# Evacuating the keys by two ScalarE operations, one directly copied head, and later stores of the first query block

## The chip, the cores and the metric

The kernel runs on one core of one Trainium2 chip. The metric is the device time of one execution in microseconds, the median of several runs. Below, PE is TensorE, DVE is VectorE, ACT is ScalarE, POOL is GpSimd, and SP is the engine whose queue issues almost all DMAs of this kernel.

## The reference

A gated mix of multi-query attention and a SwiGLU feed-forward on the same input, all in float32:

```python
def _A_ref(x, wq, wk, wv, wo):                 # 2048 tokens, 32 heads of 16, one key/value head
    q = transpose((x @ wq).reshape(B, S, H, Dh), 0, 2, 1, 3)
    k = x @ wk
    v = x @ wv
    scores = einsum("bhqd,bkd->bhqk", q, k) * (Dh ** -0.5)
    o = einsum("bhqk,bkd->bhqd", softmax(scores, -1), v)
    return transpose(o, 0, 2, 1, 3).reshape(B, S, H * Dh) @ wo

def _B_ref(x, w_gate, w_up, w_down):           # 512 -> 1792 -> 512
    return (silu(x @ w_gate) * (x @ w_up)) @ w_down

g = sigmoid((x * gate_w).sum(-1, keepdims=True))
return g * _A_ref(x, ...) + (1 - g) * _B_ref(x, ...)
```

x has 2048 rows of 512.

## The kernel before, in words

**Split numbers.** Most matmuls run in the chip's rounded float32 type. Each operand is split into a high part (the rounded value) and a low part (the rest), and a product is three matmuls: high by high, low by high, high by low. So a projection of 512 tokens (a chunk `c`; there are four) to 128 columns is 12 matmuls of 128x128 by 128x512, accumulated in one bank of PSUM, a tile `pf` of which there are three.

**The opening.** For each chunk `transpose_x` loads x, transposes it on PE (16 small matmuls per half chunk) into a PSUM tile `pss`, and splits it into `xh` (ACT) and `xl` (DVE). `project_kv` projects the chunk on keys, values and the gate together, on 113 output partitions. The key appears several times, because scores are also made of split parts: in `ks`, partitions 0 to 47 and 64 to 111 hold high, high, low of the keys, and partitions of ones hold -1. The values and the gate go through `vz` and a transposition (`transpose_v`) into `vaug`. `nk` collects the largest size of each key component, and `spread_k` brings it by one matmul into `kmax`; a query row times `kmax` bounds its scores, so that the softmax needs no maximum of its own.

**The query projection** goes in four blocks `m` of 128 columns (eight heads). `query(m, c)` makes the 12 matmuls, and its `keep` takes the bank out as `hh` (high), `hl` (low) and `qb` (the bound, size times `kmax`), and stores the three to DRAM (`q_d`). Block 0 is projected before the loop over heads begins. For the heads in `QS`, in the kernel before heads 0 and 1, their 16 rows of each part are also copied straight from these tiles into `qs`, the tile from which the scores are made, four copies for each head and chunk. The other heads are read back from `q_d` by `load_head`.

**The loop over heads** (`score`, `mix`) goes over 512 units (head by key tile of 128). A unit takes 4 score matmuls of 64 rows (two run beside each other), two exponentials of 128x1024 on ACT, and 8 small matmuls that multiply by the values. Between them PE works off a queue of jobs, cut in halves of 64 rows: eight steps for every two units, in this order: the queries of blocks 1 to 3, then the feed-forward (gate, up, down), then output parts. What is left after the loop is done at full width. `fill(GAP)` makes some of these jobs at full width before the loop: it takes jobs of 12 matmuls until GAP is used up.

**What sets the order.** Within the opening and the loop the order is as written; each engine works its instructions in program order and waits by semaphores. SP's queue is in order too: a DMA whose source is not ready holds those behind it. Two engines that read one PSUM tile do so one after the other, by waits that the compiler adds. Loads of weights that stand between the two regions are placed by a scheduler, and so may be issued earlier than they are written. `load_split` loads a weight into one of two `wraw` buffers and POOL splits it.

Of the kernel before, what the change touches and what calls it, by code (L numbers as in the profile page):

```python
# [8 lines left out]
F32 = mybir.dt.float32  # L9
F32R = mybir.dt.float32r  # L10
BF16 = mybir.dt.bfloat16
I32 = mybir.dt.int32
AF = mybir.ActivationFunctionType
# [5 lines left out]
P = 128  # L19
# [20 lines left out]
SPOT = 16  # L40
SLACK = 6
LONG = 8
GAP = 24
RATE = 8
FIRST = 5
STOP = 5
# [5 lines left out]
def tile_gated_mix(ctx, tc, x, wq, wk, wv, wo, w_gate, w_up, w_down, gate_w, out):  # L52
# [48 lines left out]
    def mm(ps, terms):  # L101
        n = len(terms)
        for i, (a, b) in enumerate(terms):
            nc.tensor.matmul(ps, a, b, start=(i == 0), stop=(i == n - 1))  # L104
# [7 lines left out]
    def run(queue, n):  # L112
        for _ in range(min(n, len(queue))):
            queue.pop(0)()
# [68 lines left out]
                run(LOADS, 2)  # L183


    WQ, QS = {}, {}

    def load_wq(m):
        WQ[m] = load_split(wq_v[:, :, m * P:(m + 1) * P], f"wq{m}", 1, qpool)

    def query(m, c):
        cs = slice(c * CH, (c + 1) * CH)
        t = m * NCH + c

        def terms():
            r = []
            for k in range(KD):
                r += three(WQ[m], XC[c], (slice(None), k), (slice(None), k))
            return r

        def keep(ps):
            qh = wp.tile([P, CH], F32R, name="hh", bufs=7)
            ql = wp.tile([P, CH], F32R, name="hl", bufs=7)

            qb = wp.tile([P, CH], F32, name="ht", bufs=2)
            if m:
                nc.vector.tensor_copy(qh, ps)
            else:
                nc.scalar.activation(qh, ps, AF.Copy)
            nc.vector.tensor_tensor(ql, ps, qh.bitcast(F32), ALU.subtract)  # L210
            if m:
                nc.vector.tensor_scalar(qb, qh.bitcast(F32), kmax, None, op0=ALU.mult)
                nc.vector.scalar_tensor_tensor(qb.bitcast(F32R), qb, -1.0, qb, op0=ALU.mult, op1=ALU.max)
            else:
                nc.scalar.activation(qb.bitcast(F32R), ps, AF.Abs, scale=kmax)
            parts = [ql, qh, qb.bitcast(F32R)]
            if not m:
                for h, qs in QS.items():
                    for i, part in enumerate([qh] + parts):
                        row = c % 2 * RT + i * DH  # L220
                        nc.sync.dma_start(qs[row:row + DH, c // 2, :].bitcast(F32), part[h * DH:(h + 1) * DH].bitcast(F32))  # L221
            for j, part in enumerate(parts):
                nc.sync.dma_start(q_d[m * HG:(m + 1) * HG, j * DH:(j + 1) * DH, cs], part.bitcast(F32))  # L223
            nc.vector.tensor_reduce(top[:, t:t + 1], qb, axis=AX.X, op=ALU.max)

        return Job(3 * KD, lambda: m in WQ, terms, keep)
# [127 lines left out]
    def whole(job):  # L354
        for i in range(job.size):
            job.step(i)
        run(ACTS, 1)
# [109 lines left out]
    def new_qs(h):  # L467
        QS[h] = qsp.tile([P, 2, CH], F32R, name="qs")
        return QS[h]

    with tc.tile_pool(name="apool", bufs=1) as ap, tc.tile_pool(name="apool2", bufs=2) as a2:
# [35 lines left out]
            nc.vector.memset(vaug[:, :, DH:], 1.0)  # L507

        nc.gpsimd.memset(ks.bitcast(F32), -1.0)
        nk = ap.tile([DH, 2 * NCH + 1], F32, name="nk")  # L510
        VZ = {}

        def transpose_x(c, i):
# [12 lines left out]
            nc.scalar.activation(hi, ptv, AF.Copy)  # L526
            nc.vector.tensor_tensor(xl[:, :, i * P:(i + 2) * P], ptv, hi.bitcast(F32), ALU.subtract)  # L527

        def project_kv(c):
            cs = slice(c * CH, (c + 1) * CH)  # L530
            if c % 2 == 0:
                VZ[c // 2] = ap.tile([KW, 2 * CH], F32, name="vz", bufs=2)
            pk = ps_f.tile([P, CH], F32, name="pf")
            terms = []
            for k in range(KD):
                terms += three((wkv_h, wkv_l), XC[c], (slice(None), k), (slice(None), k))
            mm(pk[:KW, :], terms)

            for r in (0, RT):
                nc.scalar.activation(ks[r:r + 3 * DH, cs], pk[r:r + 3 * DH, :], AF.Copy)  # L540
                lo = slice(r + 2 * DH, r + 3 * DH)
                nc.vector.tensor_tensor(ks[lo, cs], pk[lo, :], ks[lo, cs].bitcast(F32), ALU.subtract)  # L542
            nc.scalar.activation(VZ[c // 2][:, c % 2 * CH:(c % 2 + 1) * CH], pk[:KW, :], AF.Copy)  # L543
            nc.vector.tensor_reduce(nk[:, c:c + 1], pk[:DH, :], axis=AX.X, op=ALU.max)  # L544
            nc.vector.tensor_reduce(nk[:, NCH + c:NCH + c + 1], pk[:DH, :], axis=AX.X, op=ALU.min)


        def spread_k():
            nc.vector.tensor_scalar(nk[:, NCH:2 * NCH], nk[:, NCH:2 * NCH], -1.0, None, op0=ALU.mult)
            nc.vector.tensor_reduce(nk[:, 2 * NCH:], nk[:, :2 * NCH], axis=AX.X, op=ALU.max)  # L550
            pn = ps_o.tile([P, CH], F32, name="po")
            nc.tensor.matmul(pn[:, 0:1], spread.rearrange("i h j -> i (h j)"), nk[:, 2 * NCH:], start=True, stop=True)
            nc.vector.tensor_copy(kmax, pn[:, 0:1])

        def transpose_v(b):
# [10 lines left out]
        with tc.manual_schedule():  # L566
            load_wq(0)
            prepare_kv()
            prepare_norms()
            transpose_x(0, 0)  # L570
            transpose_x(0, 2)
            load_x(2, 2)
            transpose_x(1, 0)
            transpose_x(1, 2)
            load_x(3, 2)
            load_wq(1)
            load_wq(2)
            load_wq(3)
            new_qs(0)
            new_qs(1)  # L580
            project_kv(0)
            transpose_x(2, 0)
            transpose_x(2, 2)
            project_kv(1)
            transpose_x(3, 0)
            transpose_x(3, 2)
            project_kv(2)
            transpose_v(0)
            project_kv(3)
            spread_k()  # L590
            for c in range(NCH):
                whole(query(0, c))
                if c == 0:
                    transpose_v(1)

                    nc.vector.tensor_scalar(g_sb, g_sb, 0.5, 0.5, op0=ALU.mult, op1=ALU.add)
                    nc.vector.tensor_scalar(c_sb, g_sb, -0.5, 0.5, op0=ALU.mult, op1=ALU.add)
            for c in (2, 3):
                for j, part in enumerate(XC[c]):
                    nc.sync.dma_start(x_d[c - 2, j], part.bitcast(F32))  # L600
            fill(GAP)


    with tc.tile_pool(name="bpool", bufs=2) as bp:
# [3 lines left out]
        def load_head(h):  # L608
            qs = new_qs(h).bitcast(F32)
            qv = q_d[h].rearrange("r (j b s) -> b r j s", b=2, s=CH)  # L610
            for b in range(2):

                nc.sync.dma_start(qs[b * RT:b * RT + DH], qv[b, DH:2 * DH])
                nc.sync.dma_start(qs[b * RT + DH:(b + 1) * RT], qv[b])
# [42 lines left out]
                LATER.extend([lambda i=i: invert(i) for i in range(TC)] + [store])  # L657

        NU = H * NT
        for n in range(2):  # L660
            load_w("g", n)
            load_w("u", n)
# [133 lines left out]
```

## Time and profile before

| | |
|---|---|
| median of 3 runs | 1426.95 us (1425.48 to 1429.1) |
| the profiled execution | 1426.36 us |
| its span, first to last instruction | 1424.1 us |
| PE busy | 1381.7 us (97%) |
| ACT busy | 1017.0 us (71%) |
| DVE busy | 539.5 us (38%) |
| POOL busy | 374.1 us (26%) |
| mean granted PE clock | 0.989 |

Times within the profile are counted from its first instruction. In rows of the timeline the columns are: start, duration, engine, line, operation, output and inputs, count, and in brackets how long the engine stood idle before and what released it. "SPq" is SP's queue while it issues a DMA. Rows of matmuls overlap: a matmul's duration is longer than the step to the next. Granted clock is the share of full speed at which PE was allowed to run.

### The profile page before, as it was taken

The numbers are of one execution on the slowest core, as the hardware profiler recorded it, in microseconds if no ns is written. First come the engines' busy times: TensorE is split into PE (matmuls) and PEld (weight loads), VectorE is DVE, ScalarE is ACT, GpSimd is POOL, SyncE is SP. The second block draws the span as 40 slices with busy tenths as digits, with TensorE's granted clock in tenths as the row PEclk, the third lists the DMA queues.
The fourth block names the chain that finished last, engine by engine and source line by source line (L and its number), as shares of the span: only waits on it lengthen the run. The fifth ranks groups of instructions, "written<-read, shape, count | busy, mean of one in ns | idle before, by whom it ended". The sixth has DMA issues, their size and how long they took to land.

```text
span 1424.1 us, 25631 instructions
## 1 busy us (share of the span) xinstructions
PE 1381.7 (97%) x10668; PEld 745.7 (52%) x10668; DVE 539.5 (38%) x746; ACT 1017.0 (71%) x1113; POOL 374.1 (26%) x388
## 2 busy tenths in 40 slices
PE   6679999999999999999999999999999999999998
PEld 5445555555555555555555555555455555555586
DVE  6225543323334324323225334234224344334356
ACT  4257788778878777777778778778778777787500
POOL 4200022124123124133123142042136152042252
PEclk9879999999999999999999999999999999999999
DMA  6364422112114023122113141132113141121134
GB/s 179 104 220 137 127 57 57 34 42 73 39 49 130 26 80 83 34 59 76 33 43 123 34 115 45 27 86 57 34 50 100 34 123 49 35 67 35 34 107 157
DMA packets 101450, 106.66 MB, mean 75 GB/s; under 512 B 10192, under 2 KB 69584, under 8 KB 99792
## 3 DMA queue, kind: packets, MB, share of 16 engines
q1 hardware_dynamic: 99744, 104.89, 25.7%
q8 instruction: 86, 1.41, 0.4%
q10 hardware_dynamic: 1584, 0.07, 0.1%
q14 instruction: 36, 0.29, 0.1%
HBM read 74.52 MB, written 29.36 MB: 73 GB/s over the span
## 4 chain that ended last, share of the span: by engine, by line
PE 94%; DVE 2%; SPq 2%; ACT 1%; DMA 1%; issue 0%; ACTq 0%
PE pf L178 38%; PE po L636 34%; PE pss L624 21%; SPq L221 1%; PE pf L104 1%; ACT pt L627 0%; SPq L223 0%; DVE xl L527 0%; DVE ks L542 0%; DMA wkv_f<-in_gate_w_dram 0%; PE pss L524 0%; ACT ks L540 0%; DVE rsb L647 0%; DVE nk L544 0%; ACT vz L543 0%
## 5 line engine op out<-in xcount | busy, mean ns | idle before, releaser
L627 ACT ACTIVATE pt<-pss 128x1024 f32<-128x1024 f32 x1024 | 966.6, 1031 | 281.4 <-PE pss L624 281.3
L636 PE MATMUL po<-pt,vaug 128*32 128x512 f32 x4096 | 495.3, 600 | 0.0
L624 PE MATMUL pss<-qs,ks 64*128 64x512 f32 x2048 | 416.6, 435 | 16.8 <-DMA qs<-ht 14.3
L624 PEld LDWEIGHTS pss<-qs,ks 64*128 64x128 f32 x2048 | 175.6, 184 | 328.2 <-ACT pt L627 257.1
L636 PEld LDWEIGHTS po<-pt,vaug 128*32 128x32 f32 x4096 | 107.0, 109 | 223.5 <-issue 221.6
L178 PE MATMUL pf<-xl,wgh 64*128 64x512 f32 (+1 forms) x436 | 166.0, 391 | 0.0
L178 PE MATMUL pf<-xh,wul 64*128 64x512 f32 (+1 forms) x436 | 164.0, 391 | 0.0
L178 PE MATMUL pf<-xh,wuh 64*128 64x512 f32 (+1 forms) x436 | 162.6, 392 | 0.0
L178 PE MATMUL pf<-xh,wgh 64*128 64x512 f32 (+1 forms) x436 | 160.3, 391 | 0.9 <-DVE ht L262 0.9
L178 PE MATMUL pf<-xh,wgl 64*128 64x512 f32 (+1 forms) x436 | 160.3, 391 | 0.0
L94 POOL CAST wgh<-wraw 128x512 fp32r<-128x512 f32 x56 | 34.6, 617 | 475.3 <-PE pf L178 258.3
L178 PE MATMUL pf<-xl,wuh 64*128 64x512 f32 (+1 forms) x436 | 158.5, 391 | 0.0
L178 PE MATMUL pf<-wdh,hh 64*128 64x512 f32 (+1 forms) x412 | 149.1, 391 | 1.1 <-DVE hs L251 0.6
L178 PE MATMUL pf<-wdl,hh 64*128 64x512 f32 (+1 forms) x412 | 147.9, 390 | 0.0
L178 PE MATMUL pf<-wdh,hl 64*128 64x512 f32 (+1 forms) x412 | 147.6, 391 | 0.0
L94 POOL CAST wuh<-wraw 128x512 fp32r<-128x512 f32 x56 | 34.2, 611 | 419.8 <-PE pf L178 391.4
L647 DVE RECIPROCAL rsb<-rsb 128x128 f32<-128x128 f32 x128 | 116.8, 933 | 1.1
L251 DVE COPY hs<-pf 128x512 f32<-128x512 f32 x56 | 38.4, 686 | 203.4 <-PE pf L178 203.2
L262 DVE TENSOR_TENSOR ht<-ht,pf 128x512 f32<-128x512 f32 x56 | 38.3, 683 | 149.1 <-PE pf L178 149.1
L257 DVE SCALAR_TENSOR_TENSOR ht<-ht,hs 128x512 f32<-128x512 f32 x56 | 44.6, 796 | 121.9 <-ACT ht L256 119.4
L178 PEld LDWEIGHTS pf<-xh,wgh 64*128 64x128 f32 (+1 forms) x436 | 80.3, 184 | 10.1 <-POOL wdh L94 1.3
L178 PEld LDWEIGHTS pf<-xh,wgl 64*128 64x128 f32 (+1 forms) x436 | 80.4, 184 | 8.6
(145 smaller groups left out, 1585.3 us busy)
## 6 DMA issues: line engine op xcount, KB each, us to landing
wraw<-in_B_w_gate_dram SPq DMA_DIRECT2D x56, 256.0 KB
wraw<-in_B_w_up_dram SPq DMA_DIRECT2D x56, 256.0 KB
wraw<-in_B_w_down_dram SPq DMA_DIRECT2D x56, 256.0 KB
qs<-q_d SPq DMA_DIRECT2D x60, 192.0 KB
q_d<-hl SPq DMA_DIRECT2D x16, 256.0 KB
q_d<-hh SPq DMA_DIRECT2D x16, 256.0 KB
q_d<-ht SPq DMA_DIRECT2D x16, 256.0 KB
o_d<-osb SPq DMA_DIRECT2D x128, 32.0 KB
```

The costliest lines, as they stand in the source:

```text
L94: eng_hi.tensor_copy(hi, src)
L104: nc.tensor.matmul(ps, a, b, start=(i == 0), stop=(i == n - 1))
L178: nc.tensor.matmul(self.ps, a, b, start=(i == 0 and not half), stop=(last and half != 0))
L221: nc.sync.dma_start(qs[row:row + DH, c // 2, :].bitcast(F32), part[h * DH:(h + 1) * DH].bitcast(F32))
L251: nc.vector.tensor_copy(g, ps)
L257: nc.vector.scalar_tensor_tensor(t[0], t[0], 1.0, g, op0=ALU.add, op1=ALU.mult)
L262: nc.vector.tensor_tensor(t[0], t[0], ps, ALU.mult)
L624: nc.tensor.matmul(ps[:, b * CH:(b + 1) * CH], ks[rows, kt * P:(kt + 1) * P], QS[h][rows, j, :], start=True, stop=True)
L627: nc.scalar.activation(PT[u][:, j * 2 * CH:(j + 1) * 2 * CH], ps, AF.Exp, scale=SCALE)
L636: nc.tensor.matmul(po[c * 2 * DH:(c + 1) * 2 * DH, :], vaug[:, kt, :], pt[:, c * CH:(c + 1) * CH], start=(kt == 0), stop=(kt == NT - 1))
L647: nc.vector.reciprocal(rsb[:, w], rsb[:, w])
```

## The change

- `project_kv`: the bank is taken out by ACT alone, once as `vz` (all 113 partitions) and once as `ka` (the sizes of the 16 key components). One DVE reduction of `ka` gives `nk`; before, two reductions of the bank gave a maximum and a minimum. The copies into `ks` and the subtraction for its low part are made by POOL from `vz`; before, ACT and DVE made them from the bank in turn.
- `spread_k` is called before the last of the 12 matmuls of the first query chunk, not before the first.
- `keep` for block 0 makes `qb` on ACT right after `hh`, and takes its buffer from two names in turn, so four buffers, where one name had two.
- Only head 0 is copied directly (`new_qs(1)` is gone); head 1 is read back by `load_head(1)` before the loop.
- The stores of block 0 to `q_d` are collected and issued after all four chunks. The stores of x's split chunks 2 and 3 (`x_d`) are issued right after each chunk's projection, before they were issued after block 0.
- The loads of `wq` blocks 1 and 2 come after the projections of the keys, that of block 3 after the stores.
- GAP is 36 and not 24: three jobs are made before the loop, not two.

```diff
-GAP = 24
+GAP = 36
...
-            qb = wp.tile([P, CH], F32, name="ht", bufs=2)
+            qb = wp.tile([P, CH], F32, name="ht" if c % 2 else "hs", bufs=2)
             if m:
                 nc.vector.tensor_copy(qh, ps)
             else:
                 nc.scalar.activation(qh, ps, AF.Copy)
+                nc.scalar.activation(qb.bitcast(F32R), ps, AF.Abs, scale=kmax)
             nc.vector.tensor_tensor(ql, ps, qh.bitcast(F32), ALU.subtract)
...
-            else:
-                nc.scalar.activation(qb.bitcast(F32R), ps, AF.Abs, scale=kmax)
...
-            for j, part in enumerate(parts):
-                nc.sync.dma_start(q_d[m * HG:(m + 1) * HG, j * DH:(j + 1) * DH, cs], part.bitcast(F32))
+
+            def store():
+                for j, part in enumerate(parts):
+                    nc.sync.dma_start(q_d[m * HG:(m + 1) * HG, j * DH:(j + 1) * DH, cs], part.bitcast(F32))
+
+            if m:
+                store()
+            else:
+                STORES.append(store)
...
+        def store_x(c):
+            for j, part in enumerate(XC[c]):
+                nc.sync.dma_start(x_d[c - 2, j], part.bitcast(F32))
...
+            vz = VZ[c // 2][:, c % 2 * CH:(c % 2 + 1) * CH]
+            nc.scalar.activation(vz, pk[:KW, :], AF.Copy)
+            ka = a2.tile([DH, CH], F32, name="ka")
+            nc.scalar.activation(ka, pk[:DH, :], AF.Abs)
+            nc.vector.tensor_reduce(nk[:, c:c + 1], ka, axis=AX.X, op=ALU.max)
 
             for r in (0, RT):
-                nc.scalar.activation(ks[r:r + 3 * DH, cs], pk[r:r + 3 * DH, :], AF.Copy)
+                nc.gpsimd.tensor_copy(ks[r:r + 3 * DH, cs], vz[r:r + 3 * DH, :])
                 lo = slice(r + 2 * DH, r + 3 * DH)
-                nc.vector.tensor_tensor(ks[lo, cs], pk[lo, :], ks[lo, cs].bitcast(F32), ALU.subtract)
-            nc.scalar.activation(VZ[c // 2][:, c % 2 * CH:(c % 2 + 1) * CH], pk[:KW, :], AF.Copy)
-            nc.vector.tensor_reduce(nk[:, c:c + 1], pk[:DH, :], axis=AX.X, op=ALU.max)
-            nc.vector.tensor_reduce(nk[:, NCH + c:NCH + c + 1], pk[:DH, :], axis=AX.X, op=ALU.min)
+                nc.gpsimd.tensor_tensor(ks[lo, cs], vz[lo, :], ks[lo, cs].bitcast(F32), ALU.subtract)
...
-            load_wq(1)
-            load_wq(2)
-            load_wq(3)
             new_qs(0)
-            new_qs(1)
...
             project_kv(2)
+            store_x(2)
             transpose_v(0)
             project_kv(3)
-            spread_k()
+            store_x(3)
+            load_wq(1)
+            load_wq(2)
             for c in range(NCH):
-                whole(query(0, c))
+                job = query(0, c)
+                for i in range(job.size):
+                    if c == 0 and i == job.size - 1:
+                        spread_k()
+                    job.step(i)
...
-            for c in (2, 3):
-                for j, part in enumerate(XC[c]):
-                    nc.sync.dma_start(x_d[c - 2, j], part.bitcast(F32))
+            run(STORES, NCH)
+            load_wq(3)
             fill(GAP)
...
         NU = H * NT
+        load_head(1)
         for n in range(2):
             load_w("g", n)
```

How it moves instructions, at the three places of which the prediction speaks. First SP's queue at the first and second query chunk. Before (`qs_225` is head 0, `qs_226` head 1, the numbers behind hh, hl and ht tell the chunk's tiles apart):

```order
L221 DMA qs_225<-ht_390 16x512
L221 DMA qs_226<-hh_388 16x512
L221 DMA qs_226<-hl_389 16x512
...
L221 DMA qs_226<-ht_390 16x512
L223 DMA q_d_69<-hl_389 8x16x512
L223 DMA q_d_69<-hh_388 8x16x512
L223 DMA q_d_69<-ht_390 8x16x512
L221 DMA qs_225<-hh_434 16x512
```

Now (`qs_207` is head 0), at the last two chunks and behind them:

```order
L220 DMA qs_207<-hs_453 16x512
L220 DMA qs_207<-hh_475 16x512
L220 DMA qs_207<-hl_476 16x512
...
L220 DMA qs_207<-ht_477 16x512
L224 DMA q_d_69<-hl_389 8x16x512
L224 DMA q_d_69<-hh_388 8x16x512
L224 DMA q_d_69<-hs_390 8x16x512
```

Head 1's copies and the stores no longer stand between one chunk's copies for head 0 and the next one's; all twelve stores follow the last copy.

Then what follows on the same queue, between the last stores that `fill` makes and the loads of the feed-forward weights:

```order
L224 DMA q_d_69<-hl_566 8x16x512
L224 DMA q_d_69<-hh_565 8x16x512
L224 DMA q_d_69<-hs_567 8x16x512
L626 DMA qs_582<-q_d_69 16x2x512
L627 DMA qs_582<-q_d_69 48x2x512
...
L119 DMA wraw_587<-in_B_w_gate_dram 128x4x128
L119 DMA wraw_593<-in_B_w_up_dram 128x4x128
```

Head 1 (`qs_582`) is read back here; before, the loads of these weights stood ahead of all query copies.

Last POOL, at the end of the keys:

```order
L555 CAST ks_78<-vz_299 48x512
L557 TENSOR_TENSOR ks_78<-vz_299,ks_78 16x512
L94 CAST wq1h_361<-wraw_359 128x512
L95 TENSOR_TENSOR wq1l_362<-wraw_359,wq1h_361 128x512
L94 CAST wq2h_367<-wraw_365 128x512
L95 TENSOR_TENSOR wq2l_368<-wraw_365,wq2h_367 128x512
```

The splits of wq blocks 1 and 2 stand behind all sixteen key operations; before, they followed that of block 0 at once, and POOL had no key operation.

More of the change, by code (lines that the diff above doesn't have):

```diff
@@ L183, in step @@
                 run(LOADS, 2)
-    WQ, QS = {}, {}
+    WQ, QS, STORES = {}, {}, []
     def load_wq(m):
@@ L509, in tile_gated_mix @@
         nc.gpsimd.memset(ks.bitcast(F32), -1.0)
-        nk = ap.tile([DH, 2 * NCH + 1], F32, name="nk")
+        nk = ap.tile([DH, NCH + 1], F32, name="nk")
         VZ = {}
@@ L537, in project_kv @@
             mm(pk[:KW, :], terms)
+            vz = VZ[c // 2][:, c % 2 * CH:(c % 2 + 1) * CH]
[3 more added lines that the diff above has]
+            nc.vector.tensor_reduce(nk[:, c:c + 1], ka, axis=AX.X, op=ALU.max)
             for r in (0, RT):
-                nc.scalar.activation(ks[r:r + 3 * DH, cs], pk[r:r + 3 * DH, :], AF.Copy)
+                nc.gpsimd.tensor_copy(ks[r:r + 3 * DH, cs], vz[r:r + 3 * DH, :])
                 lo = slice(r + 2 * DH, r + 3 * DH)
-                nc.vector.tensor_tensor(ks[lo, cs], pk[lo, :], ks[lo, cs].bitcast(F32), ALU.subtract)
-            nc.scalar.activation(VZ[c // 2][:, c % 2 * CH:(c % 2 + 1) * CH], pk[:KW, :], AF.Copy)
-            nc.vector.tensor_reduce(nk[:, c:c + 1], pk[:DH, :], axis=AX.X, op=ALU.max)
-            nc.vector.tensor_reduce(nk[:, NCH + c:NCH + c + 1], pk[:DH, :], axis=AX.X, op=ALU.min)
+                nc.gpsimd.tensor_tensor(ks[lo, cs], vz[lo, :], ks[lo, cs].bitcast(F32), ALU.subtract)
         def spread_k():
-            nc.vector.tensor_scalar(nk[:, NCH:2 * NCH], nk[:, NCH:2 * NCH], -1.0, None, op0=ALU.mult)
-            nc.vector.tensor_reduce(nk[:, 2 * NCH:], nk[:, :2 * NCH], axis=AX.X, op=ALU.max)
+            nc.vector.tensor_reduce(nk[:, NCH:], nk[:, :NCH], axis=AX.X, op=ALU.max)
             pn = ps_o.tile([P, CH], F32, name="po")
-            nc.tensor.matmul(pn[:, 0:1], spread.rearrange("i h j -> i (h j)"), nk[:, 2 * NCH:], start=True, stop=True)
+            nc.tensor.matmul(pn[:, 0:1], spread.rearrange("i h j -> i (h j)"), nk[:, NCH:], start=True, stop=True)
             nc.vector.tensor_copy(kmax, pn[:, 0:1])
```

## The prediction

> **What bounds the kernel now.** I read the page first: the busy shares, the 40 slices and the costliest groups.
>
> ```profile
> PE 1381.7 (97%) x10668; PEld 745.7 (52%) x10668; DVE 539.5 (38%) x746; ACT 1017.0 (71%) x1113; POOL 374.1 (26%) x388
> ...
> PE   6679999999999999999999999999999999999998
> ...
> PEclk9879999999999999999999999999999999999999
> ...
> L627 ACT ACTIVATE pt<-pss 128x1024 f32<-128x1024 f32 x1024 | 966.6, 1031 | 281.4 <-PE pss L624 281.3
> ```
>
> From the fourth slice on TensorE is full, and the exponentials of ScalarE, its nearest rival, wait for it. So nothing is won in the loop over heads except by removing TensorE work, and the change removes none. The 42.4 us in which PE is not busy (1424.1 - 1381.7) lie in the first three slices (35.6 us each) and at the end. The change touches the first, so I followed the chain of waits through the first 100 us:
>
> ```profile
> 39.53 0.58 PE po L552 x2
> 40.11 4.79 PE pf L178 x12
> ...
> 50.64 0.77 SPq L223
> ...
> 62.25 1.25 SPq L221
> ...
> 75.41 2.21 DMA qs<-ht
> ...
> 77.75 0.78 PE pss L624
> ...
> 88.26 0.73 PE pss L624 x4
> ...
> 91.35 1.85 PE po L636 x16
> 93.21 0.67 PE pss L624 x4
> ```
>
> Until 39.5 the chain runs over the evacuation of the keys, then over the first query projection, and from 48 to 77.6 over the SP queue, issue after issue, until head 0's last rows have landed. Only then can the score of the fourth query chunk run. At 88.26 the first pass of the loop is done; the next takes 4.95 us (to 93.21). The gap costs clock too. Windows (PE, PEld, DVE, ACT, POOL busy, then granted clock, DMA share, GB/s):
>
> ```profile
> 64.00:66.00 2.00, 0.00 (x0) 0.00 (x0) 0.00 (x0) 0.00 (x0) 0.00 (x0) 0.62 0.64 199
> 84.00:88.00 4.00, 4.00 (x18) 0.59 (x16) 1.67 (x3) 1.07 (x2) 0.00 (x0) 0.50 1.02 405
> 96.00:114.00 18.00, 18.00 (x152) 9.04 (x150) 6.41 (x10) 13.52 (x15) 0.00 (x0) 1.00 0.49 166
> ```
>
> The first pass ran at half clock.
>
> **The keys.** Rows of the timeline, one of each kind:
>
> ```profile
> 15.97 1.91 PE L524 MATMUL pss<-ident,xt 128*128 128x128 f32 x16
> 16.24 0.59 ACT L540 ACTIVATE ks<-pf 48x512 fp32r<-48x512 f32 x1 [1.88 <-PE pf L104]
> ...
> 16.86 0.68 DVE L542 TENSOR_TENSOR ks<-pf,ks 16x512 fp32r<-16x512 f32 x1 [1.25 <-ACT ks L540]
> ...
> 18.93 0.60 ACT L543 ACTIVATE vz<-pf 113x512 f32<-113x512 f32 x1 [0.76 <-DVE ks L542]
> ...
> 19.43 1.94 ACT L526 ACTIVATE xh<-pss 128x1024 fp32r<-128x1024 f32 x2
> 19.56 0.68 DVE L544 TENSOR_REDUCE nk<-pf 16x1 f32<-16x512 f32 x1 [0.66 <-ACT vz L543]
> ...
> 19.61 0.61 POOL L94 CAST wq1h<-wraw 128x512 fp32r<-128x512 f32 x1 [6.31 <-DMA wraw<-in_A_wq_dram]
> ...
> 20.31 1.27 POOL L95 TENSOR_TENSOR wq1l<-wraw,wq1h 128x512 fp32r<-128x512 f32 x1
> ...
> 20.87 2.36 DVE L527 TENSOR_TENSOR xl<-pss,xh 128x1024 fp32r<-128x1024 f32 x2
> ...
> 28.54 0.99 PE L558 MATMUL pss<-ident,vz 113*128 113x113 f32 x8 [1.39 <-DVE xl L527]
> ...
> 39.32 0.15 DVE L550 TENSOR_REDUCE nk<-nk 16x1 f32<-16x8 f32 x1
> ...
> 51.00 0.39 PE L178 MATMUL pf<-xh,wq0h 128*128 128x512 f32 x1
> ...
> 53.72 0.39 PE L178 MATMUL pf<-xh,wq1h 128*128 128x512 f32 x1
> ```
>
> ScalarE and VectorE hand the keys' bank to each other five times before the next chunk's xh can start: the bank is full at 16.2, xh starts at 19.43 and xl ends at 23.2, 7 us for a chunk whose TensorE work is 1.91 (transposes) + 2.8 (12 matmuls). The 12 matmuls of a query chunk give their price: 53.72 - 51.00 = 2.72 us.
>
> Now ScalarE does vz (0.60) and ka (0.59, taken as the 48x512 copy's), VectorE one reduce (0.68) beside it. From the bank full at 16.2: vz and ka to 17.45, xh to 19.4, xl to 20.9. TensorE: chunk 1's projection 17.9 to 20.7, chunk 3's transposes to 22.6 (their second half needs xl at 20.9), chunk 2's projection to 25.4, the transposes of v (0.99) to 26.4, chunk 3's projection to 29.2; its xl is done at 25.4 by the same steps. TensorE sets the pace. The first query chunk's eleven matmuls end at 31.7, while vz, ka, reduce and the small maximum (0.60 + 0.59 + 0.68 + 0.15, from 29.4) end at 31.5: the norm's matmul costs its 0.58 and no wait. First chunk done: 32.5, before 44.9 (40.11 + 4.79).
>
> POOL gets two pairs of copy and subtraction for each chunk, on 48 and 16 partitions, which no row shows. Its rows on 128 partitions and the same 512 columns took 0.61 and 1.27. Cheaper than these would win nothing, because nobody waits; dearer has no row, and I bound it by twice. I take the rows: 16 operations, 15.0 us. In order, with vz of the chunks at 16.9, 21.4, 26.0 and 30.0, POOL ends the keys at 33.9, then splits wq1 to 35.8 and wq2 to 37.7. wq1 is wanted at 41.6, wq2 four chunks of work after it, wq3 later still. If the keys cost double, that cover is gone (rival 2).
>
> The x_d stores now start at 19.4. They are 4.2 MB; at 405 GB/s (84 to 88, where they ran) 10.4 us, so with the last issued at 25.5 they and wq1 behind them land by about 32. The x loads they could disturb are in before 19.6, since wq1's split, queued behind them, starts there.
>
> **The query copies.**
>
> ```profile
> 44.92 0.60 ACT L209 ACTIVATE hh<-pf 128x512 fp32r<-128x512 f32 x1 [7.32 <-PE pf L178]
> ...
> 45.55 0.69 DVE L210 TENSOR_TENSOR hl<-pf,hh 128x512 fp32r<-128x512 f32 x1 [5.24 <-ACT hh L209]
> ...
> 50.01 0.59 SPq L221 DMA_DIRECT2D qs<-ht  x1
> 50.64 0.77 SPq L223 DMA_DIRECT2D q_d<-hl  x1
> ...
> 58.56 0.69 ACT L215 ACTIVATE ht<-pf,kmax 128x512 fp32r<-128x512 f32 x1 [6.76 <-DMA q_d<-ht]
> ...
> 68.30 0.76 PE L624 MATMUL pss<-qs,ks 64*128 64x512 f32 x1 [5.57 <-DMA qs<-ht]
> ```
>
> Per chunk SP issued eight copies (0.59) and three stores (0.6 to 0.8), about 6.9 us against 2.72 of TensorE; and ScalarE stood 6.76 us at 58.56 for the store of an ht buffer. Four chunks from 45.5 gave 32 us. Now 4 issues, 2.4 us, fit under 2.72, and four buffers (two hs, two ht) end the wait. TensorE: from 32.5, transposes of v to 33.4, three chunks (8.2) to 41.6. The last chunk's hh, hs/ht and hl (0.60, 0.69, 0.69 and hand-overs) end at 43.8, its last copy is issued at 45.6 and lands about 1.7 us later (75.41 + 2.21 = 77.62, less the issue): 47.3. The fill, now three jobs, runs 41.6 to 49.8 and covers it by 2.5 us. Without it TensorE would wait 5.7.
>
> **First pass.** From 49.8: four exponentials one after another (1.03 each, the first 0.55 after its score), the last done at 54.4, then 16 mixes (1.85): 56.4, against 88.26, a gain of 31.9. At half clock, as in the row of before, it would take 10.5 (77.75 to 88.26) and end at 60.3; that is the other bound. I take the warm value, since no gap like the 5.57 us ahead of 68.30 stands there. The Trainium skill (TensorE: Matmul & The Clock Gate, part 1) says that an idle window of about 3.4 us halves the clock; the trace agrees as far as the fall to 0.62 in 64 to 66 shows. By it the start stays warm and the sum is the same; without it the 60.3 would hold.
>
> **The third fill job** takes 2.7 us of matmuls out of what is left after the loop: 12 x 0.227 = 2.7 us less there.
>
> **The stores now later.** Twelve q_d stores go out from 45.6, then nine of the next block as their values come. At 166 GB/s (96 to 114) a store of 262 KB takes 1.6 us. VectorE waits for the third before it can reuse hs (about 52); behind it stands the evacuation of two banks, which TensorE wants at about 58. I set 1.0 us for that and for hand-overs, between 0 and 4.
>
> Sum: 31.9 + 2.7 - 1.0 = 33.6 us. The profiled execution took 1426.36 us (span 1424.1 and 2.3 around it), the median is 0.6 above: 1426.36 - 33.6 = 1392.8, as a median **1393.4 us**.
>
> **Rivals.**
>
> 1. Head 1 comes late. A narrower window of stores alone (time, clock, DMA share, GB/s):
>
> ```profile
> 100.00:102.00 2.00, 1.00 0.57 195
> ```
>
> It is now read back from DRAM behind 21 stores: 45.6 + 2 + 21 x 1.6 = 81, and some 4 us for 512 KB of its own: 85. Its first score is due at 56.4 + 6 x 4.95 = 86 and a little. For it: stores and DVE waits are that tight, and the DMA share was 0.49 while only stores ran. Against it: some windows of the same stretch reached 195 GB/s, by which 81 becomes 76. Price 2 to 8 us: about 1398. The Trainium skill (DMA: Bandwidth & Descriptors, Rules for kernel authors) says that an outermost dimension below 16 holds a DMA to as many engines; these stores have 8, and the share of 0.49 agrees. By it the rate cannot rise and this rival stands; the sum, made with the measured 166, is the same.
>
> 2. POOL is slower on the keys: at twice the price it ends them at 49, wq1 at 51; TensorE stands 9.3 us and comes back cold (3 to 4 us): about 1405.
>
> 3. The first pass is cold, or copies land after 49.8: 4 us, 1397.5.
>
> 4. Slower than before: the feed-forward weights, until now issued from 23 to 44 us, stand on SP behind head 1.
>
> ```profile
> 23.52 0.37 SPq L119 DMA_DIRECT2D wraw<-in_B_w_gate_dram  x1
> ...
> 34.57 9.75 SPq L119 DMA_DIRECT2D wraw<-in_B_w_down_dram  x5
> ```
>
> Nine query jobs of 12 steps at 8 a pass last 13.5 passes, to about 123 us. If the weights come later, a pass loses 1.85 us of matmuls to the end, and can shorten only to ScalarE's 4 x 1.03 = 4.1 us: 1 us lost a pass. It takes 34 such passes, 140 us of lateness, to eat the gain: about 1430 if the weights came after 260 us. By the queue they come at 65 to 95.
>
> 5. The change does nothing: the score's start is set by something that I do not see, say a wait of the first exponential for old buffers. 1427.
>
> **How the numbers follow.** Forecast 0.64, rival 1 0.17, rival 2 0.07, rival 3 0.08, rival 4 0.02, rival 5 0.02. The forecast alone spans 1390 to 1396 (0 to 4 us for the stores, and the scatter of the runs shown, 2 us); the range reaches over rivals 1 and 3 to 1403. A measurement tells about 0.3%, 4.3 us, from no change: faster 0.96, same 0.02, slower 0.02.
>
> **What would show it.** In the profile after: the first query chunk's matmuls end near 32.5; no PE row waits for longer than 2 us between 20 and 57; the clock is 1.00 from 14 on; the first score stands at 49 to 51 behind the third fill job and waits for no copy; the first mixes end at 56 to 58; POOL ends the keys by 35; no PE wait for a head's qs at 80 to 95. Wrong: a wait of TensorE for wq1, for qs or for a bank in that stretch, or a pass that is longer than 4.95 us later on.

## The result, and the profile after

The changed kernel takes 1389.72 us (median of four runs, 1389.33 to 1394.96), the kernel before 1427.78 beside it (1425.48 to 1429.1): ratio 0.9744, 95% interval 0.9717 to 0.9771. Times 1426.95, the median shown ahead of the prediction, that is 1390.4. Timed a second time it took 1390.39 (1389.27 to 1390.79), ratio 0.9751 [0.9738, 0.9765]. The forecast was 1393.4 with a range from 1390: the direction and the mechanism came out, and the size is 3 to 4 us larger, at the range's lower end.

The page of the kernel after, the rows that answer to those of before:

```profile
PE 1372.2 (99%) x10671; PEld 741.8 (53%) x10671; DVE 525.5 (38%) x733; ACT 1013.8 (73%) x1109; POOL 388.2 (28%) x404
...
PE   8999999999999999999999999999999999999998
...
PEclk9999999999999999999999999999999999999999
...
L640 ACT ACTIVATE pt<-pss 128x1024 f32<-128x1024 f32 x1024 | 966.2, 1031 | 270.5 <-PE pss L637 262.9
```

The sixes and the seven in TensorE's first slices are gone, and so is the 7 in its clock. TensorE's idle time fell from 42.4 to 15.4 us (1387.6 - 1372.2), its busy time by 9.5 (1381.7 to 1372.2), together the 36.5 by which the span is shorter. The exponentials take the same 966 us; no operation of the loop got faster.

The chain of waits of after through the first 100 us:

```profile
28.46 2.51 PE pf L178 x11
...
31.71 0.78 PE pss L569 x8
32.49 9.42 PE pf L178 x42
41.91 7.49 issue
...
49.48 1.95 ACT pt L640 x2
...
54.29 1.85 PE po L649 x16
56.15 0.67 PE pss L637 x4
```

From 9.5 us on this chain is TensorE: no evacuation of keys, no SP issue and no landing copy stands in it, except for the exponentials of the first pass. (`issue` from 41.91 is TensorE too: the timeline shows it busy there with the rest of the three fill jobs, until 48.78, and then with the first scores.) The first mixes end at 56.15 against 88.26.

Where the 36.5 us went is read from windows cut at the same two events in both kernels, the end of the first mixes and the end of the last ones (us, then PE, PEld, DVE, ACT and POOL busy, granted clock, DMA share, GB/s). Before:

```profile
0.00:88.26 88.26, 55.72 (x240) 39.80 (x240) 36.99 (x72) 27.50 (x39) 27.00 (x34) 0.83 0.52 154
88.26:1340.23 1251.97, 1248.13 (x10093) 643.00 (x10093) 453.00 (x608) 987.56 (x1071) 317.63 (x326) 1.00 0.24 67
```

After:

```profile
0.00:56.15 56.15, 49.32 (x252) 38.41 (x252) 27.69 (x57) 24.37 (x35) 23.33 (x30) 1.00 0.63 207
56.15:1306.72 1250.57, 1248.42 (x10099) 643.31 (x10099) 450.66 (x612) 987.50 (x1071) 334.87 (x346) 1.00 0.25 68
```

The start gives 88.26 - 56.15 = 32.1 us (25.7 of it idle time of TensorE, 6.4 work that ran at half speed, in the first query chunk and the first pass, less what the third fill job adds); the loop 1.4; what follows the loop 83.87 (1424.1 - 1340.23) against 80.88 (1387.6 - 1306.72), 3.0. Sum 36.5.

### The profile page after: what moved, and what is told of

It is laid out like the page before. It is cut to its first block, busy times and chain, and to the rows that moved or that the text cites. A ratio compares the mean times of both kernels' runs of the same rounds, so it can differ in the third digit from the quotient of the medians.

```text
span 1387.6 us, 25617 instructions
## 1 busy us (share of the span) xinstructions
PE 1372.2 (99%) x10671; PEld 741.8 (53%) x10671; DVE 525.5 (38%) x733; ACT 1013.8 (73%) x1109; POOL 388.2 (28%) x404
## 4 chain that ended last, share of the span: by engine, by line
PE 98%; issue 1%; ACT 0%; DVE 0%; DMA 0%; ACTq 0%
PE pf L178 39%; PE po L649 34%; PE pss L637 22%; PE pf L104 2%; PE pss L530 1%; ACT pt L640 0%; DMA wkv_f<-in_gate_w_dram 0%; PE pss L569 0%; DVE xl L533 0%; DVE rsb L660 0%; DVE rsb L656 0%; DVE os L440 0%; DVE osb L654 0%; DVE hs L257 0%; ACTq L489 0%
## 5 line engine op out<-in xcount | busy, mean ns | idle before, releaser
L178 PEld LDWEIGHTS pf<-xl,wgh 64*128 64x128 f32 (+1 forms) x436 | 80.4, 184 | 8.2
```

Source lines behind the costliest of these rows:

```text
L178: nc.tensor.matmul(self.ps, a, b, start=(i == 0 and not half), stop=(last and half != 0))
```

## The experiments

**The keys as before, all else changed.**

```diff
-            nc.scalar.activation(vz, pk[:KW, :], AF.Copy)
-            nc.scalar.activation(ka, pk[:DH, :], AF.Abs)
-            nc.vector.tensor_reduce(nk[:, c:c + 1], ka, axis=AX.X, op=ALU.max)
             for r in (0, RT):
-                nc.gpsimd.tensor_copy(ks[r:r + 3 * DH, cs], vz[r:r + 3 * DH, :])
-                nc.gpsimd.tensor_tensor(ks[lo, cs], vz[lo, :], ks[lo, cs].bitcast(F32), ALU.subtract)
+                nc.scalar.activation(ks[r:r + 3 * DH, cs], pk[r:r + 3 * DH, :], AF.Copy)
+                nc.vector.tensor_tensor(ks[lo, cs], pk[lo, :], ks[lo, cs].bitcast(F32), ALU.subtract)
+            nc.scalar.activation(VZ[c // 2][:, c % 2 * CH:(c % 2 + 1) * CH], pk[:KW, :], AF.Copy)
+            nc.vector.tensor_reduce(nk[:, c:c + 1], pk[:DH, :], axis=AX.X, op=ALU.max)
+            nc.vector.tensor_reduce(nk[:, NCH + c:NCH + c + 1], pk[:DH, :], axis=AX.X, op=ALU.min)
...
```

> The changed kernel with the evacuation of the keys as before (ScalarE and VectorE take the bank in turns, two reductions), everything else changed. My theory: the keys and the query copies are two gates in series, each paid in full. The keys' chain then ends at about 39.5 us as before, the first query chunk at about 40.5 instead of 31.7, and everything behind it moves by 8 to 11 us: a span of 1396 to 1399 us, where the changed kernel has 1387.6. Rival: the copies alone were the gate, and the keys lay beside them: not over 2 us more than the changed kernel, 1388 to 1390.

Measured: 1401.52, ratio 0.9825 [0.9807, 0.9843], 11 to 12 us above the changed kernel, more than expected. The end of its keys in the chain of waits, and the first pass:

```profile
36.08 0.60 ACT ks L550
...
36.71 0.71 DVE ks L552
...
37.44 0.61 ACT vz L553
...
38.06 0.68 DVE nk L554
...
41.38 0.73 PE pf L178
...
66.38 2.78 PE po L648 x16
```

The hand-overs between ScalarE and VectorE stand in the chain again, and the first query chunk ends at 42.1 (41.38 + 0.73) instead of 31.7: 10.4 us (0.65 of it because its first key projection began at 13.42 and not at 12.77). The first mixes end at 69.16 instead of 56.15, 13.0 later. The other 2.6 are clock: 1.1 behind the norm, where the clock is at 0.50 from 38 to 44, and 1.5 in the first pass, where these 16 mixes took 2.78 instead of 1.85 and the window 64 to 66 has a granted clock of 0.71. So the key gain reaches the end, as long as the queries' copies no longer set it.

**The new keys alone, in the kernel before.** Only the evacuation is edited; loads, copies and stores stay.

```diff
-                nc.scalar.activation(ks[r:r + 3 * DH, cs], pk[r:r + 3 * DH, :], AF.Copy)
+                nc.gpsimd.tensor_copy(ks[r:r + 3 * DH, cs], vz[r:r + 3 * DH, :])
...
-                nc.vector.tensor_tensor(ks[lo, cs], pk[lo, :], ks[lo, cs].bitcast(F32), ALU.subtract)
+                nc.gpsimd.tensor_tensor(ks[lo, cs], vz[lo, :], ks[lo, cs].bitcast(F32), ALU.subtract)
...
```

> The kernel before with the new evacuation of the keys alone. Two gates in series: the first query chunk ends 9 to 11 us earlier, and the issues on SP behind it, which keep their 32 us, move with it: 9 to 12 us less than before, a span of 1412 to 1415. Rival (the copies alone were the gate): no more than 2 us less, 1422 to 1424. Second rival (the gain needs both): less than half of 10 us here and less than half there.

Measured: 1430.87, ratio 1.0033 [1.0021, 1.0045]: slower, where I expected 9 to 12 us less. My theory fell here. POOL and then SP in its timeline:

```profile
46.26 1.27 POOL L548 TENSOR_TENSOR ks<-vz,ks 16x512 fp32r<-16x512 f32 x1
47.58 0.61 POOL L546 CAST ks<-vz 48x512 fp32r<-48x512 f32 x1
48.27 1.26 POOL L95 TENSOR_TENSOR wul<-wraw,wuh 128x512 fp32r<-128x512 f32 x1
```

```profile
43.62 6.27 SPq L119 DMA_DIRECT2D wraw<-in_B_w_down_dram  x2
49.95 0.64 SPq L221 DMA_DIRECT2D qs<-hh  x1
```

The first query chunk is ready 8.7 us earlier (36.2 against 44.9), but its copies start at 49.95, in the kernel before it was 45.54. The key operations and the splits of weights take turns on POOL; a weight load on SP waits until a split has freed one of the two `wraw` buffers; and the query copies stand behind that load. The change put the weight loads behind the keys as well, which I had described and not priced as a condition.

**That condition, tested: loads moved, with the old and with the new keys.** Both are the kernel before with wq1 and wq2 loaded after the last keys, wq3 after the x_d stores, and the feed-forward weights' loads put inside the section whose order is kept as written:

```diff
-            load_wq(1)
-            load_wq(2)
-            load_wq(3)
             new_qs(0)
...
             project_kv(3)
+            load_wq(1)
+            load_wq(2)
...
                     nc.sync.dma_start(x_d[c - 2, j], part.bitcast(F32))
+            load_wq(3)
             fill(GAP)
...
+        with tc.manual_schedule():
             for n in range(2):
                 load_w("g", n)
                 load_w("u", n)
             for n in GROUPS[0]:
                 load_w("d", n)
-        with tc.manual_schedule():
             score(0, 0)
```

Old keys:

> The kernel before with the same moved loads and its old evacuation of the keys. Theory: nothing waits for these weights in the first 90 us of the kernel before, so the time is that of before within 0.3% (1424 to 1431). Rival: the loads alone are worth something, since four fewer issues and transfers stand ahead of the query copies: 2 to 5 less.

New keys:

> The kernel before, with the new evacuation of the keys, and with the loads of the weights set behind: wq1 and wq2 after the last keys, wq3 behind the x_d stores, the FFN's weights behind that, written so that they cannot stand earlier on SP or POOL. Theory (the keys alone gained nothing because their POOL operations were mixed with the splits of those weights, and SP stood at a weight load in front of the query copies): the first query chunk ends some 10 us earlier, as the 10.4 us between 42.1 with the old evacuation and 31.7 in the changed kernel say, both heads' copies and the stores go out some 9 to 10 us earlier, the first mixes of the loop end at 78 to 80 instead of 88.26, and the time is 9 to 11 us below the kernel before: 1416 to 1419, ratio 0.992 to 0.994. Rival (the copies' queue is limited by something else than when the query chunks are ready, such as the x_d stores or the copies' own rate): 0 to 4 less, 1423 to 1428.

Measured: 1442.74 with the old keys (ratio 1.0118 [1.01, 1.0136]) and 1435.67 with the new ones (1.0064 [1.0042, 1.0087]). Neither expectation held as a time, because the late loads cost something that I had not seen. The longest of TensorE's waits between 20 and 200 us, with the new keys:

```profile
PE po L638 <- DVE osb L643: 15.2, 1, 15.2
```

With the old keys it is 14.4 us. Its origin, on VectorE in the kernel with the new keys:

```profile
126.08 0.48 DVE L212 TENSOR_SCALAR ht<-hh,kmax 128x512 f32<-128x512 f32 x1 [18.72 <-DMA q_d<-ht]
...
131.78 0.68 DVE L643 COPY osb<-po 128x512 f32<-128x512 f32 x1
```

The weight loads stand together on SP, behind 4 MB of x_d stores, each waiting for a split. Stores of the second query block stand behind them; VectorE waits 18.72 us for one of these before it reuses ht; and head 0's output, which it has to evacuate, waits behind that. But the step in question did work: the first mixes end at 79.6 (75.91 + 3.64) with the new keys and at 88.8 (85.14 + 3.64) with the old, and the two medians differ by 7.1 us.

**The hold taken away: x_d stores under the keys too.**

```diff
             project_kv(2)
+            store_x(2)
             transpose_v(0)
             project_kv(3)
+            store_x(3)
...
-            for c in (2, 3):
-                for j, part in enumerate(XC[c]):
-                    nc.sync.dma_start(x_d[c - 2, j], part.bitcast(F32))
             load_wq(3)
```

> As the kernel with the new keys and the late loads, and the four x_d stores go out under the keys, as in the changed kernel. With the x_d stores between the copies and the weights, wq3's load took 14.1 us, the FFN's loads and the second block's stores stood behind one another on SP, VectorE was held 18.72 us (126.08) for a store, and TensorE waited 15.2 us for the evacuation of head 0's output; without that wait the time would have been about 1420. Theory (the earlier keys are worth the 9 us by which the first mixes end earlier, 79.5 against 88.3, once nothing takes them back): the last copy of head 0 lands at 68 to 70 as before, the wait for osb is gone, 1414 to 1420, ratio 0.992 to 0.996. Rival (the loads of the FFN's weights, two buffers and 2 us of POOL each, hold up SP wherever they stand close together): TensorE still waits 5 to 15 us for osb, 1422 to 1433.

Measured: 1419.09 (1416.41 to 1422.78), ratio 0.9955 [0.9939, 0.9972]: as the theory said. In its trace TensorE waits 1.3 us for osb; the first mixes end at 78.3. This kernel still copies two heads directly and stores between the chunks, so its score still waits for copies:

```profile
58.73 0.76 PE L629 MATMUL pss<-qs,ks 64*128 64x512 f32 x1 [5.45 <-DMA qs<-ht]
67.76 1.22 PE L629 MATMUL pss<-qs,ks 64*128 64x512 f32 x3 [8.27 <-DMA qs<-ht]
```

Thus, the evacuation with its moved loads and x_d stores is worth 4 to 9 us of the 1426.76 measured beside it, and what is left of the change (one head copied, stores behind, third fill job, the norm's place, four buffers) the other 29. The two parts do not simply add: with everything else changed, the keys were worth 11 to 12.

**Both heads copied directly, all else changed.**

```diff
             new_qs(0)
+            new_qs(1)
...
-        load_head(1)
```

> The changed kernel with head 1 copied directly too (eight copies a chunk, and no reading back of head 1); the stores stay behind the copies. SP then issues 8 x 0.6 = 4.8 us a chunk against 2.72 us of TensorE: the last copy for head 0 is issued at about 49 and lands at about 50.7, 2 us behind the fill's end at 48.6: 2 to 4 us more than the changed kernel, a span of 1389.5 to 1391.5. Rival (the number of copies is the whole of the old delay): over 10 us more. Second rival (the fill covers it): the same within 0.5 us.

Measured: 1397.0 (1395.55 to 1398.92), ratio 0.9794 [0.9774, 0.9814], 6.6 to 7.3 above the two timings of the changed kernel; expected were 2 to 4. Some 1.9 us of the profiled one is that its first query matmul came at 30.39 instead of 28.46. TensorE's wait for copies, and VectorE's hold for a store:

```profile
54.62 1.19 PE L638 MATMUL pss<-qs,ks 64*128 64x512 f32 x3 [3.17 <-DMA qs<-ht]
```

```profile
63.27 0.48 DVE L213 TENSOR_SCALAR hs<-hh,kmax 128x512 f32<-128x512 f32 x1 [16.47 <-DMA q_d<-hs]
```

The wait of 3.17 us brings the half clock with it: granted 0.50 from 54 to 62, and the 16 mixes take 2.8 us. I had priced the wait and not the clock. Head 1's sixteen issues also push the first store back to 55.7, and VectorE's hold grows from 7.10 to 16.47 us; TensorE waits 0.77 us for a bank behind it.

**The first block's stores between the chunks' copies.**

```diff
-            if m:
-                store()
-            else:
-                STORES.append(store)
+            store()
```

> The changed kernel with the stores of block 0 issued between the chunks' copies, as before; one head copied, four buffers. SP issues 4 copies and 3 stores a chunk, 4.4 us, and copies stand behind stores in the DMA queues: the last copy is issued at about 48 to 49 and lands 2 to 5 us later, at 50 to 54: 2 to 8 us more than the changed kernel (with a cold TensorE at the upper end), a span of 1389.5 to 1395.5. Rival (stores are hidden whatever their place): the same within 0.5 us.

Measured: 1400.46 (1399.45 to 1401.49), ratio 0.9819 [0.9802, 0.9837], 10 to 11 more; expected were 2 to 8. SP at the third chunk:

```profile
42.77 0.60 SPq L224 DMA_DIRECT2D q_d<-ht  x1
43.48 1.24 SPq L220 DMA_DIRECT2D qs<-hh  x1
44.81 2.14 SPq L220 DMA_DIRECT2D qs<-hl  x1
47.00 0.57 SPq L220 DMA_DIRECT2D qs<-hh  x1
```

A chunk's three stores (0.67, 0.67 and 0.60) cost SP not these 1.9 us but 4.2: the two issues behind them take 1.24 and 2.14 us instead of about 0.55. A chunk then lasts 6.9 us on SP (43.48 to 50.40) against 2.72 on TensorE, the last copy leaves at 54.60 instead of 43.89, TensorE waits 6.38 us for it, and the clock is 0.50 until 64. My expectation had priced the stores by their own rows. The same two slow issues follow the stores in the kernel before the change (1.23 and 2.11 us at 52.85 and 54.17), whose later chunks took 9.4 us each on SP (52.85 to 62.25) and not the 6.9 that the prediction added up from its rows.

**Two fill jobs instead of three.**

```diff
-GAP = 36
+GAP = 24
```

> The changed kernel with two jobs before the loop instead of three. The last copy lands at about 46.1 (issued until 44.4, 1.7 us), the fill ends at 46.0: TensorE waits next to nothing, the first score moves forward by 2.5 us, and the third job comes back at the end with 2.7 us. My theory: the third job only fills a gap, so it is worth what gap is left, 0 to 1 us: a span of 1387.5 to 1388.6. Rival, which is how the term of my sum can also be read (a job made ahead saves its 2.7 us): 2 to 3 us more, 1389.5 to 1390.6.

Measured: 1393.73 (1393.06 to 1395.02), ratio 0.9774 [0.976, 0.9787]. Both readings missed. No copy is late: the first scores start at 46.32 instead of 48.78 and wait for no copy, so the third job was not needed to cover the copies. Yet the first mixes end at 56.37, 0.2 later than in the changed kernel (its keys ended 0.26 later as well):

```profile
52.80 3.57 PE po L649 x16
```

```profile
51.00:56.00 5.00, 5.00 (x22) 1.47 (x20) 3.15 (x5) 2.05 (x2) 0.00 (x0) 0.50 0.52 199
```

The first pass ran at half clock, and its head start of 2.5 us went into that. The profiled run, the slowest of its five, is 5.9 us longer than that of the changed kernel timed beside it (1393.3 against 1387.4): 0.4 of it has come by the end of the first mixes, 2.3 come in the loop, and 3.3 behind it, where the job not done ahead is made. In the loop TensorE waits for VectorE in two places of the feed-forward:

```profile
PE pf L178 <- DVE ht L268: 1.4, 2, 0.9
PE pf L178 <- DVE hs L257: 0.6, 1, 0.6
```

The kernel before has these waits too (1.4 and 0.6). So the third job saves more than its own matmuls.

**The job behind the first scores.** If TensorE's idle time in the first pass is what costs, a job that runs there gives it something to do.

```diff
-GAP = 36
+GAP = 24
...
             score(0, 0)
             score(0, 1)
+            fill(3 * KD)
```

> The changed kernel with two jobs before the first score and the third behind the two scores of unit 0. The changed kernel's first pass leaves TensorE idle for about 1.5 us (1.04 and 0.42 at 50.6 and 51.5, waiting for the first exponentials). The third job would lie over these exponentials: 1 to 1.5 us less than the changed kernel, a span of 1386.0 to 1386.8. Rival: the copies land later than 46.0 or the second pair of scores waits anyway, no gain, 1387.3 to 1388.

Measured: 1389.09 (1386.38 to 1389.77), ratio 0.9735 [0.972, 0.975], 1.3 below the changed kernel timed beside it (0.9751 [0.9738, 0.9765]). The intervals overlap, so the timing does not separate the two. The chain shows the step itself:

```profile
30.15 2.51 PE pf L178 x11
...
47.82 0.66 PE pss L637 x4
48.49 2.94 PE pf L178 x12
...
54.41 1.85 PE po L649 x16
```

TensorE waits for nothing between 26 and 110, the clock stays at 1.00, and the first mixes end 26.1 us after the first query matmul, in the changed kernel 27.7 (56.15 - 28.46).

**The norm's matmul ahead of the first query chunk.**

```diff
+            spread_k()
             for c in range(NCH):
                 job = query(0, c)
                 for i in range(job.size):
-                    if c == 0 and i == job.size - 1:
-                        spread_k()
                     job.step(i)
```

> The changed kernel with the norm's matmul before the first query chunk, as before. TensorE is ready for it at about 28.4, the last reduction ends at 30.5: TensorE stands 2.2 us, and all behind it moves: 1.8 to 2.4 us more than the changed kernel, a span of 1389.4 to 1390.2. Rival (the fill's cover takes it up): the same within 0.5 us.

Measured: 1393.75 (1390.74 to 1396.73), ratio 0.9776 [0.9758, 0.9794]. TensorE waits 2.0 us for the last chunk's reduce and the norm, and only then starts the first query chunk; its row in the chain:

```profile
29.89 2.99 PE pf L178 x12
```

In the profiled run the first chunk is done at 32.88, 1.2 us later than in the changed kernel, although its first key projection began 1.0 earlier (11.76 against 12.77): the step costs 2.2 us, as expected. The pass stays warm, and the span is 2.6 above that of the changed kernel timed beside it. The median is 3.4 above; the runs scatter by 6 us, and no trace shows what the slower ones did.

**The x_d stores behind the first block's stores.**

```diff
             project_kv(2)
-            store_x(2)
             transpose_v(0)
             project_kv(3)
-            store_x(3)
...
             run(STORES, NCH)
+            store_x(2)
+            store_x(3)
             load_wq(3)
```

> The changed kernel with its four x_d stores (2 chunks, 2 parts) moved from under the keys to behind the first block's stores, ahead of the load of wq3 and of head 1's reads. Theory: these 4 MB (four parts of 1 MB) then lie between the stores of the first block and head 1's rows, at 200 to 390 GB/s 10 to 20 us, so head 1 lands at about 90 instead of about 80 and the score that is due at 87 waits: 2 to 6 us more, 1392 to 1396. Rival: the queue has slack for them, head 1 is still in time, and the time is that of the changed kernel to 0.5 us.

Measured: 1395.21 (1394.41 to 1396.91), ratio 0.979 [0.9773, 0.9808], 4.8 to 5.5 above the changed kernel, as the theory said (some 1.1 us of the profiled one is a later first query matmul). Head 1 is read back behind 4 MB more, and TensorE waits for it:

```profile
91.02 0.46 PE L637 MATMUL pss<-qs,ks 64*128 64x512 f32 x1 [2.69 <-DMA qs<-q_d]
```

In the changed kernel the same score runs at 87.16 and waits for nothing; POOL's split at 80.05, which waited for a load that was issued behind head 1, suggests about 7 us of room there. So placing these stores under the keys, which the prediction only priced for harm, is what keeps rival 1 away.

That head 0's late stores need the two buffer names was not tried by taking them back: with two buffers and the stores behind all copies, the third chunk's values would wait for a store that stands behind their own copies on SP, by the order of the code a deadlock.

## Why the prediction was right, and where it was off

**The keys** came out step by step. Rows of after:

```profile
15.83 0.60 ACT L549 ACTIVATE vz<-pf 113x512 f32<-113x512 f32 x1 [1.75 <-PE pf L104]
16.32 0.57 ACT L551 ACTIVATE ka<-pf 16x512 f32<-16x512 f32 x1
16.80 1.91 ACT L532 ACTIVATE xh<-pss 128x1024 fp32r<-128x1024 f32 x2
```

```profile
31.61 0.61 POOL L555 CAST ks<-vz 48x512 fp32r<-48x512 f32 x1
32.31 1.29 POOL L557 TENSOR_TENSOR ks<-vz,ks 16x512 fp32r<-16x512 f32 x1
33.66 0.61 POOL L94 CAST wq1h<-wraw 128x512 fp32r<-128x512 f32 x1
```

xh follows 0.97 us after vz began, the time taken for ka was 0.59 and is 0.57. POOL's price on 48 and 16 partitions is that of 128 (0.61 and 1.29, taken 0.61 and 1.27), and it ends the keys at 33.6 (predicted 33.9). Rival 2 is out. What the step lacked is the condition: it held because POOL and SP were free of weights. The kernel with the new keys alone, 4.6 us slower than the one before timed beside it, shows that I had the right number without the reason that carried it.

**The query copies** left SP as worked out, about 1 us earlier: the first query chunk is done at 32.49 less the transposes, 31.7 (predicted 32.5), and the last copy is issued at 43.89 + 0.54 = 44.4 (45.6).

**The first pass** started at 48.78 (predicted 49.8) and stayed warm. Its end at 56.15 against 56.4 gives 32.1 for the predicted 31.9. That it came so near is in part luck, in two ways. First, two errors cancel: the pass began 1.0 us earlier and took 7.4 us instead of 6.6. I let the mixes follow the fourth exponential; that one ended at 53.25 (49.48 + 3.77), but TensorE still had steps of the job queue and scores to do, and its mixes began at 54.29. Second, the reason given for the warm start does not carry it. I argued that no gap ahead of the scores was left. With two fill jobs there is none either, the two waits in the pass are the same 1.04 and 0.42 us, and the clock fell all the same. With the keys as before all three fill jobs stand ahead, the waits are 0.97 and 0.42, and the clock fell there too (0.50 from 65 to 68). So rival 3 is real, and my argument did not rule it out; a cold pass itself cost 2.7 us (10.05 instead of 7.37, two fill jobs) and 1.5 (8.85, keys as before), and not the 4 that I gave.

**The third fill job** was put too low. I had 2.7 us; what follows the loop is 3.0 shorter and has 15 matmuls fewer in the chain (141 + 147 against 138 + 135), of which 12 were foreseen:

```profile
1306.72 32.07 PE pf L178 x138
1338.91 31.06 PE pf L178 x135
```

**The stores now later** is a term that failed. I took 1.0 us off for VectorE's hold and hand-overs. The hold came where it was predicted (about 52):

```profile
51.96 0.49 DVE L213 TENSOR_SCALAR hs<-hh,kmax 128x512 f32<-128x512 f32 x1 [7.10 <-DMA q_d<-hs]
```

TensorE never waited for it. Between 50 and 1310 its waits in after are four for exponentials, two in the first pass and two at the loop's end, and one more:

```profile
PE pss L637 <- ACT pt L640: 2.8, 4, 1.0
PE pf L178 <- DVE hs L257: 0.7, 1, 0.7
```

Instead of costing 1.0, the loop gained 1.4. TensorE's busy time in the two windows above differs by 0.3 us, its idle time fell from 3.84 to 2.15 (1251.97 - 1248.13 and 1250.57 - 1248.42). Of waits between the first pass and the loop's end, before has 2.0 us (1.4 for ht, 0.6 for hs, in the feed-forward jobs) and after 0.7. What moved these waits is the third fill job: the kernel with two fill jobs differs from the changed one in nothing else, and has the 2.0 again and an idle time of 3.90 in its loop (1252.78 - 1248.88). All six kernels with two jobs, that before among them, have 2.0 or 2.1 us of these waits for ht and hs; the other eight wait 0.6 to 1.1 us there. Why a job's place moves them is open. So, by these traces, the 1.4 belongs to the third fill job, which was worth 4.4 (3.0 and 1.4) and not 2.7, and the stores' term is 0. In the profiled runs 33.6 thus became 36.5: 0.2 more at the start, 1.7 more by the third fill job, and 1.0 not lost to the stores.

**Rival 1**, head 1 late, was the right one to weigh most, and its rate was at the fast end. After, where stores alone run:

```profile
50.00:60.00 10.00, 9.02 (x56) 5.01 (x60) 6.30 (x10) 8.52 (x10) 0.00 (x0) 1.00 0.52 197
```

At 197 GB/s the bound of 76 for the end of the stores was nearer than the 81 that I took. Head 1's reads were issued from 71.16, a load issued behind them had landed by 80.05, and head 1 was wanted at 87.16. The Trainium skill (DMA: Bandwidth & Descriptors, Rules for kernel authors) says that an outermost dimension below 16 holds a DMA to as many engines; the share of 0.52, with stores whose outermost dimension is 8, agrees.

**Rival 4**, slower through late feed-forward weights, did not come here: the first was issued at 75.00, as worked out. But as a mechanism it is real, by another path than I gave. In the two kernels with late loads behind the x_d stores the weights themselves were not missed; they held the stores on SP, these held VectorE, and that cost TensorE 14 to 15 us.

## What to carry to other kernels

An operation that is moved to a free engine brings along everything that is already queued there: here the moved key operations lost time until the weight splits, and the loads that wait for those splits, were put behind them. On one in-order issue queue, price a group of transfers by when the next transfer leaves, not by its own rows, and put what TensorE waits for first. When the wait at the start of a pipeline is nearly gone, filler behind the first scores rather than ahead of them keeps the engine from idling in the first pass; here one trace shows this, and the timing does not separate it.

## What the runs showed of the hardware that I had not expected

- The two copies behind three stores took SP 1.24 and 2.14 us to issue, against 0.54 to 0.58 for those after them. In every kernel with stores between copies the first of the two takes 1.22 to 1.26 us and the second 1.32 to 2.14.
- TensorE's clock fell to 0.50 behind two idle times of only 1.04 and 0.42 us (two fill jobs, from 51) and of 0.97 and 0.42 (the keys as before, three fill jobs, from 65). It stayed at 1.00 behind 1.04 and 0.42 in the changed kernel and 1.04 and 0.41 in that with the norm first. The 3 us that hold both waits do not tell them apart: TensorE is busy 1.53 and 1.61 of them where the clock fell (47 to 50 and 61 to 64), 1.54 and 1.55 where it did not (49 to 52 and 50 to 53). What decides between them is open. The Trainium skill (TensorE: Matmul & The Clock Gate, part 1) speaks of an idle window of about 3.4 us that runs freely, so that the same work can meet it differently from run to run. The differing outcomes agree with that; that no window of this length was idle here, and the clock still fell, does not.
- One of the four timed runs of the changed kernel took 1394.96 us at a mean granted clock of 0.995 instead of 0.999. It is 5 us more than the other three, and the traced first passes at half clock cost 1.5 and 2.7; there is no trace of this run, and its cause is open.
- The start of the work moves from run to run: the first query matmul stands at 28.46 in the changed kernel, at 27.32 and 30.15 in kernels whose instructions up to there are the same.
